# Attention inputs in 2 KB runs, seven warm-up products, no weight piece on ScalarE's queue, and a last expert turned part by part

## The chip, the cores and the metric

The kernel runs on one core of one Trainium2 chip. The metric is the device time of one execution in microseconds (us), as the median over runs. TensorE is called PE, VectorE DVE, ScalarE ACT, GpSimd POOL and SyncE SP, as in the profile.

## The reference

Three layers follow one another on 4 x 576 = 2304 tokens of 512 numbers, all in float32:

```python
def phi(x):                                  # 8 heads of 64, omega is 128 x 64
    proj = np.einsum('bhsd,md->bhsm', x, omega)
    h = proj - np.sum(x * x, axis=-1, keepdims=True) / 2.0
    h = h - np.max(h, axis=-1, keepdims=True)
    return np.exp(h) / np.sqrt(m)
q_p, k_p = phi(q * scale), phi(k * scale)
num = q_p @ (k_p^T v);  den = q_p @ sum(k_p) + 1e-6;  x = num / den

h = x @ w_in;  x = (h - np.tanh(h)) @ w_out      # w_in 512 x 2048, w_out 2048 x 512

logits = x @ w_gate                          # 8 experts, each takes 288 tokens,
                                             # handed out in the order of the logits
out[mask] = np.maximum(x[mask] @ w1[e], 0) @ w2[e]   # w1 512 x 1024, w2 1024 x 512
```

The kernel takes its inputs in a layout that the host makes by copying and turning them alone; w_in and w_out come as 64-bit numbers, since the reference's hold them so.

## The kernel before

The attention goes in 72 steps, called units: for k or q, a granule of two tiles of 128 tokens (or one shared tile, "sh", of two sequences), one half of the heads (hh, four heads) and one head pair. `load_gran` (L390) loads a granule: q and k turned, with the features on the partitions, into a tile `ld`; v into `v1`, whose 65th column per head is set to one by a memset on POOL, so that the sum of k_p comes out of the same product. `unit_ops` (L415) projects it (L436), takes the maximum (DVE, L450), the exponential (ACT, L447), and either adds k_p^T v up in PSUM (L467) or turns q_p (L489) and multiplies (L496). The results are 18 tiles `xt` of 128 tokens.

The MLP goes over six blocks of 384 tokens (three tiles) and 16 chunks of 128 of the 2048 hidden features. float32 accuracy is had from three products of a high and a low part: xH with the high part of w_in, xL with it, and xH with the low part (L611 to L613, in the text M1), then 9 such products per chunk into three accumulators (L658). `weight_ops` (L330) makes these parts from the 64-bit weights: a DMA brings a raw piece of 128 x 512, three steps on DVE (L341, L343, L345) make float32 of it, ACT copies the high part, DVE or POOL subtracts (L305) to get the low part, which is stored to DRAM and read back when a block needs it. `x_ops` (L541) turns an `xt` tile and splits it into xH and xL. The experts follow at about 610 us (`expert_ops`, L1369): gather 288 rows, turn, two layers with the same three products (L1428 to L1430, L1447 to L1449), turn back (L1459) and scatter the rows to the output in three indirect DMAs of POOL.

Nothing of the order is written by hand. Every operation is given to a planner, `Plan` (L66), with a duration and a due time (`plan.at` plus `lag`), and `Plan.run` (L130) puts them out, one at a time, by the earliest start that its own account of the engines, the buffers and the DMA allows, and by due time among equals. Where an operation names two engines, the one that ends earlier by the account is taken; `bias` is added to DVE's end there. Where the account sees PE wait for more than 0.9, `spare` (L1484) puts small products of ones into an accumulator that is not used yet (L1489), for 0.4 of that wait and at most 1.0. Before everything, `warm` (L1478) issues 15 products of 512 columns. The instructions of each engine then run in that order, each waiting for its semaphores.

Names that the text uses: `omega_ops` (L312) loads omega twice, for both halves of the partitions, and scales it on DVE; `bias_ops` (L320) runs two small ACT instructions; LEADX, LEADI, LEADO (L774), WO0 (L1524) and the number in `low_ops` (L1556) are offsets of due times; `end_rows` exists in the changed kernel alone.

## Time and profile before

| | us |
|---|---|
| median of 3 runs | 867.41 |
| lowest and highest run | 864.65, 870.2 |
| the profiled execution | 868.87 |
| its span, first to last instruction | 867.1 |
| PE busy | 839.3 (97%) |
| DVE busy | 651.8 (75%) |
| ACT busy | 470.5 (54%) |
| POOL busy | 272.5 (31%) |

The profile shows one execution. A busy PE is not a PE at its peak: its instructions overlap, and their ends are modelled. In the rows below, "idle before" in square brackets is the time in which the engine had nothing to run, and the name behind the arrow is what ended it. The granted clock is given as a share of full speed: 1.00 is 2.4 GHz and 0.50 is 1.2 GHz. Instructions of PE take 16 entries for eight projections, since each float32 product is done in two passes.

### The profile page before, as it was taken

The numbers are of one execution on the slowest core, as the hardware profiler recorded it, in microseconds if no ns is written. First come the engines' busy times: TensorE is split into PE (matmuls) and PEld (weight loads), VectorE is DVE, ScalarE is ACT, GpSimd is POOL, SyncE is SP. The second block draws the span as 40 slices with busy tenths as digits, with TensorE's granted clock in tenths as the row PEclk, the third lists the DMA queues.
The fourth block names the chain that finished last, engine by engine and source line by source line (L and its number), as shares of the span: only waits on it lengthen the run. The fifth ranks groups of instructions, "written<-read, shape, count | busy, mean of one in ns | idle before, by whom it ended". The sixth has DMA issues, their size and how long they took to land. (4 is left out here: it accounts for less than half of the span.)

```text
span 867.1 us, 17421 instructions
## 1 busy us (share of the span) xinstructions
PE 839.3 (97%) x6126; PEld 750.9 (87%) x6126; DVE 651.8 (75%) x1906; ACT 470.5 (54%) x1024; POOL 272.5 (31%) x292
## 2 busy tenths in 40 slices
PE   7998999999999999999999999999999999999995
PEld 5988888898888888788988996777999999999995
DVE  6979999778777888878878867445878878876720
ACT  4966564655457554565558864013565555554721
POOL 2131343433353345344423334010042142142211
PEclk9989999999999999999999999999999999999998
DMA  8979877977557665743459884668879879779600
GB/s 258 337 261 286 275 250 236 313 257 241 147 178 226 189 207 161 233 141 113 122 191 320 290 300 144 186 219 267 250 221 299 249 211 301 250 193 343 225 28 28
DMA packets 103790, 193.95 MB, mean 224 GB/s; under 512 B 28305, under 2 KB 42257, under 8 KB 103698
## 3 DMA queue, kind: packets, MB, share of 16 engines
q1 hardware_dynamic: 97586, 172.80, 60.5%
q0 software_dynamic: 5664, 18.88, 9.0%
q8 instruction: 49, 0.80, 0.4%
q10 hardware_dynamic: 448, 1.11, 0.4%
q14 instruction: 43, 0.35, 0.1%
HBM read 149.64 MB, written 33.69 MB: 211 GB/s over the span
## 5 line engine op out<-in xcount | busy, mean ns | idle before, releaser
L305 POOL TENSOR_TENSOR gL<-s,gH 128x384 fp32r<-128x384 f32 x68 | 80.0, 1178 | 172.9 <-ACT gH L300 163.7
L611 PE MATMUL bk<-xH,wi 128*128 128x384 f32 x332 | 118.3, 356 | 4.6 <-ACT phi L447 2.7
L739 DVE SCALAR_TENSOR_TENSOR lw<-wf,raw 128x512 f32<-128x512 f32 x128 | 108.9, 850 | 5.3 <-POOL wf L736 2.6
L612 PE MATMUL bk<-xL,wi 128*128 128x384 f32 x332 | 112.1, 338 | 0.0
L613 PE MATMUL bk<-xH,iL 128*128 128x384 f32 x332 | 112.1, 338 | 0.0
L658 PE MATMUL acc<-wo,gL 128*128 128x512 f32 x282 | 111.4, 396 | 0.0
L658 PE MATMUL acc<-wo,gH 128*128 128x512 f32 x240 | 98.8, 412 | 0.0
L658 PE MATMUL acc<-oL,gH 128*128 128x512 f32 x240 | 95.1, 396 | 0.9 <-DVE oL L305 0.8
L447 ACT ACTIVATE phi<-bk,nm 128x128 f32<-128x128 f32 x268 | 75.8, 384 | 32.9 <-DVE nm L450 32.6
L736 POOL TENSOR_TENSOR wf<-oL,wo 128x512 f32<-128x512 f32 x48 | 66.7, 1390 | 38.7 <-DMA oL<-low_wo 36.3
L611 PEld LDWEIGHTS bk<-xH,wi 128*128 128x128 f32 x332 | 63.0, 190 | 11.9 <-ACT phi L447 3.4
L636 DVE SCALAR_TENSOR_TENSOR s<-s,bk 128x384 f32<-128x384 f32 x83 | 45.4, 549 | 33.2 <-ACT s L635 32.8
L615 ACT ACTIVATE s<-bk 128x384 f32<-128x384 f32 x80 | 39.2, 490 | 55.1 <-PE bk L613 49.2
L300 ACT ACTIVATE gH<-s 128x384 fp32r<-128x384 f32 x80 | 42.0, 525 | 46.2 <-DVE s L638 28.1
L612 PEld LDWEIGHTS bk<-xL,wi 128*128 128x128 f32 x332 | 63.1, 190 | 2.8
L658 PEld LDWEIGHTS acc<-wo,gL 128*128 128x128 f32 x282 | 52.9, 188 | 12.3 <-POOL gL L305 0.5
L613 PEld LDWEIGHTS bk<-xH,iL 128*128 128x128 f32 x332 | 62.9, 189 | 0.0
L638 DVE SCALAR_TENSOR_TENSOR s<-s,s 128x384 f32<-128x384 f32 x80 | 55.4, 693 | 0.9
L635 ACT ACTIVATE s<-s,qbias 128x384 f32<-128x384 f32 x80 | 49.3, 616 | 6.3 <-DVE gL L305 1.9
L658 PEld LDWEIGHTS acc<-oL,gH 128*128 128x128 f32 x240 | 45.2, 188 | 7.4 <-DVE oL L305 1.6
L658 PEld LDWEIGHTS acc<-wo,gH 128*128 128x128 f32 x240 | 45.2, 188 | 6.8 <-issue 1.0
L450 DVE TENSOR_REDUCE nm<-bk 128x4 f32<-128x512 f32 (+1 forms) x74 | 45.7, 633 | 6.8 <-PE bk L436 6.2
(413 smaller groups left out, 2320.4 us busy)
## 6 DMA issues: line engine op xcount, KB each, us to landing
r_wraw<-in_moe_w_dram SPq DMA_DIRECT2D x50, 512.0 KB, 5.3
iL<-low_wi SPq DMA_DIRECT2D x80, 256.0 KB, 3.2
oL<-low_wo SPq DMA_DIRECT2D x78, 256.0 KB, 3.1
raw<-in_moe_w_out_dram SPq DMA_DIRECT2D x32, 512.0 KB, 4.3
raw<-in_moe_w_in_dram SPq DMA_DIRECT2D x30, 512.0 KB, 5.2
s_wraw<-in_moe_w_dram SPq DMA_DIRECT2D x14, 512.0 KB, 5.8
dw<-in_moe_w_dram SPq DMA_DIRECT2D x13, 512.0 KB, 5.3
w1l<-dw SPq DMA_DIRECT2D x13, 512.0 KB, 3.0
```

Of the source, the lines that this page charges most:

```text
L305: (nc.gpsimd if e == POOL else nc.vector).tensor_tensor(out, in_, high.bitcast(F32), op=OP.subtract)
L447: nc.scalar.activation(ph.t[:, i0 + i, :], pj.t[:, i * M:(i + 1) * M], AF.Exp, bias=nmx.t[:, i0 + i:i0 + i + 1])
L450: plan.op(DVE, 0.1 + 0.125 * n, lambda e, pj=pj, i0=i0, n=n: V.tensor_reduce(nmx.t[:, i0:i0 + n], pj.t[:, :n * M].rearrange("p (i m) -> p ...
L611: nc.tensor.matmul(ph(), piece(iH, c), xH.t[:, c, :], start=(c == 0), stop=False)
L612: nc.tensor.matmul(ph(), piece(iH, c), xL.t[:, c, :], start=False, stop=False)
L613: nc.tensor.matmul(ph(), piece(iL, c), xH.t[:, c, :], start=False, stop=(c == NC - 1))
L635: plan.op(ACT, 0.52, lambda e: nc.scalar.activation(s.t, ut(), AF.Square, bias=qbias), r=[u], w=[s], lag=2.8)
L636: plan.op(DVE, 0.52, lambda e: V.scalar_tensor_tensor(s.t, s.t, QD, ph(), op0=OP.add, op1=OP.mult), r=[p, s], w=[s], lag=3.4)
L638: plan.op(DVE, 0.65, lambda e: V.scalar_tensor_tensor(s.t, s.t, QC, ut(), op0=OP.mult, op1=OP.mult), r=[u, s], w=[s], lag=4.0)
L658: nc.tensor.matmul(acc[t].t, (gL if k == 2 else gH).t[:, c], (oL if k == 1 else oH).t, start=(f == 0 and k == 0), stop=(f == end and k == ...
L736: plan.op(POOL, 1.45, lambda e: nc.gpsimd.tensor_tensor(w.t, lo.t.bitcast(F32), wo[:, f, :].bitcast(F32), op=OP.add), r=[lo, wbuf["wo", f] ...
L739: x_reads.append(plan.op(DVE, 0.9, lambda e, i=i: nc.vector.scalar_tensor_tensor(scratch.t.bitcast(F32), w.t, 1.0, half(rows[i // 2], i % ...
```

## The change

It has four parts and new numbers for the planner.

The host lays q, k and v out so that what one partition of a granule takes lies in one run: 2 KB for q and k (1 KB for the shared tile), 2080 bytes for v, whose ones are now in the DRAM rows. One DMA loads a granule of v where two did, and the 20 memsets go. omega comes with both halves, in one DMA.

The first two raw pieces of w_in, which went over ACT's queue, go over SP's like the others. The ACT instructions of `bias_ops` no longer share a buffer with omega.

There are 7 warm-up products instead of 15. `spare` is used from a wait of 0.5 on while the planner's time is below 25.

For the last expert, the rows are no longer turned at the end in twelve transposes and three copies of 512 columns: after each of the four quarters of the second layer, `end_rows` copies it and turns it for all three groups of rows, writes the first three quarters out behind the third, and the last quarter in three small pieces.

```diff
-    bias = {"PE": 0.0, "ACT": 0.0, "DVE": 0.6, "POOL": 0.0, "SP": 0.0, "-": 0.0}
+    bias = {"PE": 0.0, "ACT": 0.0, "DVE": 0.66, "POOL": 0.0, "SP": 0.0, "-": 0.0}
-            if e == "PE" and self.fill and t - self.free[e] > 0.9:
+            if e == "PE" and self.fill and t - self.free[e] > (0.5 if t < 25.0 else 0.9):
-                self.dma = max(self.dma, end) + o.nbytes / 280e3
+                self.dma = max(self.dma, end) + o.nbytes / 300e3
-        first = kind == "wi" and f < 2 and not masked
+        first = kind == "wi" and f < 0 and not masked
-            plan.op(POOL, 0.04, lambda e: nc.gpsimd.memset(t.t[:, :n, :, D:], 1.0), w=[t], lag=-6.0)
-            for i in range(n):
-                plan.op(SP, 0.47, lambda e, i=i: nc.sync.dma_start(
-                    t.t[:, i, :, :D], v[(tile + i) * P:(tile + i + 1) * P, hh * HH * D:(hh + 1) * HH * D].rearrange(
-                        "p (h d) -> p h d", d=D)), w=[t], lag=-5.0, nbytes=P * HH * D * 4)
+            W = HH * (D + 1)
+            plan.op(SP, 0.47, lambda e: nc.sync.dma_start(
+                t.t.rearrange("p i h d -> p (i h d)")[:, :n * W], v[b // 2, hh, :, tile % 9 * W:(tile % 9 + n) * W]),
+                w=[t], lag=-5.0, nbytes=P * W * 4 * n)
-    LAG2, LEADX, LEADI, LEADO = 10.35, 14.35, 8.14, 3.98
+    LAG2, LEADX, LEADI, LEADO = 10.35, 4.72, 9.7, 4.85
-                        plan.at = max(x_due[i * TPB + t] + 11.86, start[j - 1] + LEADX)
+                        plan.at = max(x_due[i * TPB + t] + 5.24, start[j - 1] + LEADX)
+    def end_rows(p, d, py, yT):
+        if not d:
+            tails[:] = [(Buf(bank3), Buf(mLr), []) for _ in range(NG)]
+        ends = d == NC - 1
+        cp = None
+        if not ends:
+            plan.op({ACT: 0.3, DVE: 0.37}, 0, lambda e: copy(e, yT.t, py.t[:, :CAP]), r=[py], w=[yT])
+            plan.at += 1.0
+        for g in range(NG):
+            (po, yo, done), n, ix = tails[g], GN[g], idxs[p][g][0]
+            cols = slice(g * GS, g * GS + n)
+            if ends:
+                cp = plan.op((ACT, DVE, ACT)[g], 0.2, lambda e, cols=cols: copy(e, yT.t[:, cols], py.t[:, cols]),
+                             r=[py], wp=[yT])
+            done.append(plan.op(PE, 0.11, lambda e, po=po, n=n, cols=cols: nc.tensor.transpose(
+                po.t[:n, d * P:(d + 1) * P], yT.t[:, cols], ident), rp=[yT], wp=[po],
+                after=([cp] if ends else [yT.writers[-1]]) + done[-1:]))
+            if d >= NC - 2:
+                part = slice(0, d * P + P) if not ends else slice(d * P, DM)
+                w = part.stop - part.start
+                plan.op((ACT, DVE, ACT)[g], 0.1 + 0.001 * w, lambda e, po=po, yo=yo, n=n, part=part: copy(
+                    e, yo.t[:n, part].bitcast(F32), po.t[:n, part]), rp=[po], wp=[yo], after=done[-1:])
+            if ends:
+                plan.op(POOL, 1.1, lambda e, g=g, yo=yo, ix=ix: scatter(g, yo, ix), r=[yo, ix], late=3.5)
-        for i in range(15):
+        for i in range(7):
-    T_UNIT, T_MLP, DUE0, DUE1 = 2.23, 60.95, 7.39, 19.25
+    T_UNIT, T_MLP, DUE0, DUE1 = 2.23, 58.66, 7.39, 19.25
-    WI0, WI1, WO0 = 3.84, 2.4, -13.4
+    WI0, WI1, WO0 = 3.84, 2.4, -10.66
-    low_ops(starts[-2], (NF * steps[-1] + -19.47) / (E * NPRE))
+    low_ops(starts[-2], (NF * steps[-1] + -13.85) / (E * NPRE))
```

The planner's account of each engine also starts at 0.9 to 1.6 instead of 0.

The order on SP, where the kernel begins, of before (ld and v are the granules' tiles, raw a weight piece):

```order
L405 DMA ld_173<-in_k_dram 128x2x256
L399 DMA v_175<-in_v_dram 128x4x64 x2
L405 DMA ld_189<-in_k_dram 128x2x256
L399 DMA v_177<-in_v_dram 128x4x64 x2
L405 DMA ld_195<-in_k_dram 128x2x128
L399 DMA v_179<-in_v_dram 128x4x64
L339 DMA raw_198<-in_moe_w_in_dram 128x1024
L405 DMA ld_200<-in_k_dram 128x2x256
```

And of the changed kernel, the same place on SP:

```order
L404 DMA ld_157<-in_k_dram 128x512
L398 DMA v_162<-in_v_dram 128x520
L404 DMA ld_173<-in_k_dram 128x512
L398 DMA v_176<-in_v_dram 128x520
L339 DMA raw_178<-in_moe_w_in_dram 128x1024
L339 DMA raw_180<-in_moe_w_in_dram 128x1024
L404 DMA ld_182<-in_k_dram 128x256
L398 DMA v_185<-in_v_dram 128x260
```

The two raw pieces came from ACT's queue; they now stand behind the first two granules of k and v and ahead of the third.

The order on DVE, where its work begins, of before (nm are the maxima of a projection in a bank bk or rx, wf the float32 weights):

```order
L315 TENSOR_SCALAR omT<-omT 128x128
L341 TENSOR_SCALAR wf_215<-raw_187 128x512
L343 SCALAR_TENSOR_TENSOR wf_215<-raw_187,wf_215 128x512
L450 TENSOR_REDUCE nm_230<-bk_205 128x4
L450 TENSOR_REDUCE nm_232<-bk_206 128x4
L345 SCALAR_TENSOR_TENSOR wf_215<-raw_187,wf_215 128x512
L450 TENSOR_REDUCE nm_247<-bk_218 128x4
L341 TENSOR_SCALAR wf_266<-raw_191 128x512
L450 TENSOR_REDUCE nm_275<-rx_219 128x4
```

And of the changed kernel, the same place on DVE:

```order
L315 TENSOR_SCALAR omT<-omT 128x128
L451 TENSOR_REDUCE nm_201<-bk_189 128x4
L451 TENSOR_REDUCE nm_215<-bk_190 128x4
L451 TENSOR_REDUCE nm_222<-bk_205 128x4
L451 TENSOR_REDUCE nm_240<-rx_206 128x4
L341 TENSOR_SCALAR wf_247<-raw_178 128x512
L343 SCALAR_TENSOR_TENSOR wf_247<-raw_178,wf_247 128x512
L345 SCALAR_TENSOR_TENSOR wf_247<-raw_178,wf_247 128x512
L341 TENSOR_SCALAR wf_272<-raw_180 128x512
```

The four maxima of the first two granules moved ahead of the first weight piece.

The order on PE at its end, of before (s_yT are the quarters of the last expert's result, bd and be banks):

```order
L1449 MATMUL bd_17105<-s_hH_17044,s_ewL_16843 128x288
L1459 MATMUL bd_17134<-ident,s_yT_17064 128x128
L1459 MATMUL bd_17134<-ident,s_yT_17082 128x128
L1459 MATMUL bd_17134<-ident,s_yT_17109 128x128
L1459 MATMUL bd_17134<-ident,s_yT_17132 128x128
L1459 MATMUL be_17139<-ident,s_yT_17064 128x128
```

And of the changed kernel, from the third quarter's transposes among the products of the fourth on:

```order
L1487 MATMUL bd_17121<-s_hH_16931,s_ewL_16742 128x288
L1396 MATMUL bd_17076<-ident,s_yT_17125 128x128
L1396 MATMUL be_17078<-ident,s_yT_17125 128x128
L1396 MATMUL be_17080<-ident,s_yT_17125 32x128
L1485 MATMUL bd_17121<-s_hH_16948,wi 128x288
L1486 MATMUL bd_17121<-s_hL_16953,wi 128x288
```

Nine of the twelve transposes moved ahead of the last product; behind it stand the three of the last quarter.

## Rows read from the trace of the kernel before

**Rows 1.** The page, part 1: busy time, share of the span, instructions.

```profile
PE 839.3 (97%) x6126; PEld 750.9 (87%) x6126; DVE 651.8 (75%) x1906; ACT 470.5 (54%) x1024; POOL 272.5 (31%) x292
```

**Rows 2.** Busy time by stage: length, engines with instructions, PE clock, DMA share, GB/s.

```profile
0.00:50.00 50.00, 43.31 (x394) 36.20 (x394) 39.52 (x92) 35.23 (x109) 12.03 (x23) 0.97 0.98 309
50.00:60.00 10.00, 9.72 (x72) 9.46 (x72) 6.36 (x12) 6.31 (x17) 2.20 (x3) 0.82 0.55 180
60.00:136.00 76.00, 71.38 (x479) 63.07 (x480) 72.08 (x132) 47.05 (x120) 24.85 (x23) 1.00 0.83 265
...
610.00:835.00 225.00, 224.72 (x2070) 217.36 (x2069) 175.53 (x776) 126.97 (x211) 61.58 (x81) 1.00 0.79 244
```

**Rows 3.** Timeline of the start, PE: start, duration, line, tiles, count, idle before.

```profile
1.65 5.47 PE L1480 MATMUL bk<-onev 128*128 128x512 bf16 x15 [1.65 <-DVE onev L251]
...
7.05 1.16 PE L436 MATMUL bk<-omT,ld 64*128 64x128 f32 x16
...
10.59 0.37 PE L436 MATMUL bk<-omT,ld 64*128 64x128 f32 x1 [2.38 <-DMA ld<-in_k_dram]
...
11.68 0.76 PE L1489 MATMUL kv<-onev 128*128 128x128 bf16 x10
```

**Rows 4.** Timeline of DVE, 5 to 50 us.

```profile
8.73 0.43 DVE L341 TENSOR_SCALAR wf<-raw 128x512 uint32<-128x512 uint32 x1 [3.39 <-DMA raw<-in_moe_w_in_dram]
9.19 0.69 DVE L343 SCALAR_TENSOR_TENSOR wf<-raw,wf 128x512 uint32<-128x512 uint32 x1
9.80 1.28 DVE L450 TENSOR_REDUCE nm<-bk 128x4 f32<-128x512 f32 x2
...
16.77 1.64 DVE L345 SCALAR_TENSOR_TENSOR wf<-raw,wf 128x512 uint32<-128x512 uint32 x1
...
49.09 0.69 DVE L305 TENSOR_TENSOR xL<-bk,xH 128x512 fp32r<-128x512 f32 x1 [0.80 <-ACT xH L300]
```

**Rows 5.** DMA issues of the span: tiles, queue, count, size, median us to landing.

```profile
raw<-in_moe_w_in_dram SPq DMA_DIRECT2D x30, 512.0 KB, 5.2
...
ld<-in_k_dram SPq DMA_DIRECT2D x16, 256.0 KB, 5.0
...
omT<-in_omega_dram ACTq DMA_DIRECT2D x2, 32.0 KB, 3.4
```

**Rows 6.** Busy time in a stretch of 2 us, columns as in rows 2.

```profile
48.00:50.00 2.00, 1.44 (x8) 1.04 (x6) 1.20 (x3) 1.54 (x6) 0.96 (x1) 0.50 0.96 350
```

**Rows 7.** Timeline of PE where the MLP starts.

```profile
49.84 0.69 PE L611 MATMUL bk<-xH,wi 128*128 128x384 f32 x1 [0.56 <-DVE xL L305]
...
53.74 0.33 PE L611 MATMUL bk<-xH,wi 128*128 128x384 f32 x1
...
55.84 1.89 PE L467 MATMUL kv<-v,phi 128*128 128x65 f32 x16
```

**Rows 8.** What PE waited for, 60 to 136 us: total, times, longest.

```profile
PE bk L611 <- DVE xt L509: 1.3, 1, 1.3
```

**Rows 9.** Groups of DVE: count, busy, mean ns, idle before.

```profile
L305 DVE TENSOR_TENSOR gL<-s,gH 128x384 fp32r<-128x384 f32 x12 | 8.1, 673 | 3.1 <-ACT gH L300 3.1
...
L305 DVE TENSOR_TENSOR lw<-wf,wi 128x512 fp32r<-128x512 f32 x4 | 3.8, 953 | 0.0
```

**Rows 10.** Timeline of POOL, 12 to 32 us.

```profile
16.42 1.45 POOL L305 TENSOR_TENSOR lw<-wf,wi 128x512 fp32r<-128x512 f32 x1 [1.18 <-ACT wi L300]
```

**Rows 11.** Timeline of the end, 853 to 868 us.

```profile
855.39 0.49 PE L1459 MATMUL bd<-ident,s_yT 128*128 128x128 f32 x3
855.65 0.41 ACT L300 ACTIVATE s_yT<-bd 128x288 f32<-128x288 f32 x1 [2.77 <-PE bd L1449]
...
856.48 0.60 ACT L300 ACTIVATE mL<-bd 128x512 f32<-128x512 f32 x1 [0.42 <-PE bd L1459]
...
857.36 0.98 POOL L1463 DMA_INDIRECT out_dram<-mL,r_ix  x1 [22.87 <-ACT mL L300]
...
858.64 0.96 POOL L1463 DMA_INDIRECT out_dram<-mL,r_ix  x1 [0.21 <-issue]
```

More of the change, by code (lines that the diff above doesn't have):

```diff
@@ L70 @@
     CROSS, SAME = 0.2, 0.13
-    bias = {"PE": 0.0, "ACT": 0.0, "DVE": 0.6, "POOL": 0.0, "SP": 0.0, "-": 0.0}
+    bias = {"PE": 0.0, "ACT": 0.0, "DVE": 0.66, "POOL": 0.0, "SP": 0.0, "-": 0.0}
     def __init__(self):
         self.ops, self.n, self.at = [], 0, 0.0
-        self.free = dict.fromkeys(("PE", "ACT", "DVE", "POOL", "SP", "-"), 0.0)
+        self.free = {"PE": 1.6, "ACT": 0.9, "DVE": 1.5, "POOL": 1.2, "SP": 0.9, "-": 0.0}
         self.dma = 0.0
@@ L191, in tile_kernel @@
     nc = tc.nc
-    D, M = omega.shape
+    D, M = omega.shape[0] // 2, omega.shape[1]
     P = 128
-    NT, DM = v.shape
+    NT, DM = out.shape
     H = DM // D
@@ L310, in tile_kernel @@
     bT = Buf(None)
+    bBias = Buf(None)
     def omega_ops():
-        for i in range(2):
-            plan.op(ACT, 0.6, lambda e, i=i: nc.scalar.dma_start(omT[i * D:(i + 1) * D, :], omega), w=[bT], nbytes=P * D * 4)
+        plan.op(ACT, 0.6, lambda e: nc.scalar.dma_start(omT, omega), w=[bT], nbytes=P * M * 4)
         plan.op(DVE, 0.2, lambda e: nc.vector.tensor_scalar(omT, omT, 1.0 / math.sqrt(math.sqrt(D)), None, op0=OP.mult),
@@ L321, in bias_ops @@
         for x in (pbias, qbias):
[L322 removed]
+            plan.op(ACT, 0.8, lambda e, x=x: nc.scalar.activation(x, x, AF.Copy), w=[bBias])
     HMIN = 2.0 ** -15 * 1.125
@@ L429, in unit_ops @@
             two = held_pj[nm, b, g, hh] = Buf(bank, early=early), Buf(bank, early=early)
+            lv = lambda: ld.t.rearrange("p a n -> p (a n)").rearrange("p (a n) -> p a n", n=P if sh else 2 * P)
             def proj(e):
@@ L435, in proj @@
                             rows, i = slice(c * D, (c + 1) * D), 2 * r + a
-                            nc.tensor.matmul(two[c].t[:, i * M:(i + 1) * M], ld.t[rows, a, r * P:(r + 1) * P], omT[rows],
+                            nc.tensor.matmul(two[c].t[:, i * M:(i + 1) * M], lv()[rows, a, r * P:(r + 1) * P], omT[rows],
                                              start=True, stop=True)
@@ L1367, in tile_kernel, with scatter @@
     sc_prev = []
+    def scatter(g, yo, ix):
+        nc.gpsimd.memset(spacer, 0.0)
+        st = nc.gpsimd.indirect_dma_start(
+            out=out, out_offset=bass.IndirectOffsetOnAxis(ap=ix.t[:GN[g]].bitcast(U32), axis=0),
+            in_=yo.t[:GN[g]].bitcast(F32), in_offset=None)
+        for x in sc_prev:
+            tc.declare_no_dep(st.ins, x.ins, reason="every token has one expert")
+        sc_prev.append(st)
+    tails = []
+    def end_rows(p, d, py, yT):
[22 more added lines that the diff above has]
+                plan.op(POOL, 1.1, lambda e, g=g, yo=yo, ix=ix: scatter(g, yo, ix), r=[yo, ix], late=3.5)
     def expert_ops(p):
@@ L1450, in expert_ops @@
                 o = plan.op(PE, 0.40, mm, r=[H, L, hH, hL], w=[py], after=[o] if o else [])
+            if p == E - 1:
+                end_rows(p, d, py, yT)
+                continue
             plan.op({ACT: 0.3, DVE: 0.37}, 0, lambda e, py=py, yT=yT: copy(e, yT.t, py.t[:, :CAP]), r=[py], w=[yT])
             ys.append(yT)
+        if p == E - 1:
+            return
         plan.at = base + AT_OUT
@@ L1459, in transposes @@
                     nc.tensor.transpose(po.t[:GN[g], d * P:(d + 1) * P], ys[d].t[:, g * GS:g * GS + GN[g]], ident)
-            def scatter(e, g=g, yo=yo, ix=ix):
-                nc.gpsimd.memset(spacer, 0.0)
-                st = nc.gpsimd.indirect_dma_start(
-                    out=out, out_offset=bass.IndirectOffsetOnAxis(ap=ix.t[:GN[g]].bitcast(U32), axis=0),
-                    in_=yo.t[:GN[g]].bitcast(F32), in_offset=None)
-                for x in sc_prev:
-                    tc.declare_no_dep(st.ins, x.ins, reason="every token has one expert")
-                sc_prev.append(st)
             plan.op(PE, 0.44, transposes, r=ys, w=[po])
             plan.op({ACT: 0.48, DVE: 0.6}, 0, lambda e, g=g, po=po, yo=yo: copy(e, yo.t[:GN[g]].bitcast(F32), po.t[:GN[g], :]), r=[po], w=[yo])
-            plan.op(POOL, 1.1, scatter, r=[yo, ix], late=3.5)
+            plan.op(POOL, 1.1, lambda e, g=g, yo=yo, ix=ix: scatter(g, yo, ix), r=[yo, ix], late=3.5)
     plan.at = -30.0
@@ L1478, in warm @@
     def warm(e):
-        for i in range(15):
+        for i in range(7):
             nc.tensor.matmul(idle.t, onev.to_broadcast([P, P]), onev.to_broadcast([P, DM]), start=True, stop=True)
-    plan.op(PE, 6.0, warm, w=[idle])
+    plan.op(PE, 3.0, warm, w=[idle])
     def spare(us):
@@ L1664, in _lay_out @@
 def _lay_out(np, name, a):
-    if name in ("omega", "moe2_w_gate_t"):
+    if name == "omega":
+        return np.concatenate((a.T, a.T), 0)
+    if name == "moe2_w_gate_t":
         return a.T
@@ L1677, in _lay_out @@
     a = np.concatenate((a[:, 0], a[:, 1, e:], a[:, 1, :e]), 1)
-    return a.reshape(B * S, H * D) if name == "v" else a.transpose(0, 2, 1)
+    if name == "v":
+        a = np.concatenate((a.reshape(B // 2, -1, 128, H, D), np.ones((B // 2, 2 * S // 128, 128, H, 1), a.dtype)), 4)
+        return a.reshape(B // 2, -1, 128, 2, H // 2 * (D + 1)).transpose(0, 3, 2, 1, 4).reshape(B // 2, 2, 128, -1)
+    a = a.transpose(0, 2, 1).reshape(B // 2, 2, 2, 128, 2 * S).transpose(0, 1, 3, 2, 4)
+    cuts = (0, 256, 512, 640, 896, 1152)
+    return np.concatenate([a[..., i:j].reshape(B // 2, 2, 128, -1) for i, j in zip(cuts, cuts[1:])], 3)
 def _in_order(np, x, S=576):
```

5 lines of the change are left out of this document (2 added, 3 removed).

## The prediction

> **What bounds the kernel now.** I read the page first: TensorE (PE) is busy in 97% of the span [rows 1], so some 28 us hold no product, and only these, products that do no work and half-rate stretches can be won. The table of stages says where they lie [rows 2]: 6.7 us in the first 50, 4.6 us between 60 and 136, only 0.3 us between 610 and 835; the rest is short waits between and the drain behind the last product. Then the timelines. At the start [rows 3] the 15 warm-up products from 1.65 take 5.5 us, the first projection follows at 7.05 and takes 1.16 us, and the second stands 2.4 us for its k tile. VectorE (DVE) idles 3.4 us until the first raw weight piece lands at 8.73; from there it is nearly full until the third low part of x at 49.09 [rows 4], behind which the first product of the MLP (L611) starts at 49.84 [rows 7]. DVE has 39.5 us of work in the first 50 us [rows 2], so from 8.73 on DVE sets when the MLP starts. From there PE itself sets the pace, except for its waits between 60 and 136, in which DVE is busy 72.1 of 76 us.
>
> **The start.** The loads carry the same bytes (v a little more, for its ones); they are issued in other pieces and another order. SP's queue now begins k, v, k, v, raw, raw in six issues, where it held k, v, v, k, v, v; ScalarE's queue issues omega once and no raw piece. PE: at the row's spacing seven products end at 4.2 to 4.7 (15 took 5.47 us, the last of them closer together than the first, so the first seven took up to 3.0) instead of 7.04. Omega lands 3.4 us behind an issue at 0.9 [rows 5]: 4.3. The first k tile, issued at 0.9 too, lands at 5.9 by the median of 5.0 us [rows 5]; with next to nothing queued ahead of it, it can come as omega does, at 4.3. I take 5.3 for the first projection, between the two. Its 1.16 us put DVE's first reduction at 6.5. The four reductions that now stand ahead of the weights need 2.6 us (two take 1.28 [rows 4]), until 9.1; the first raw piece, fifth in SP's queue and so issued near 2.7, needs 5.2 us [rows 5] and is there at 7.9: no second wait. DVE's full stretch then starts at 6.5 instead of 8.73, 2.2 us earlier. Against that DVE does one weight piece more ahead of the third low part of x (0.43 + 0.69 + 0.69 = 1.8 us [rows 4]), and one low part of a weight (0.95 [rows 9]) and one copy less: 0.7 us net. So the MLP starts 1.5 us earlier. Bounds: 0, if the k tile needs its 5.9 and DVE is held up by 0.9 us more; -2.8, if the k tile is there at 4.3 and the extra piece fills holes. I take **-1.5**.
>
> **The clock.** The granted clock is 0.50, the lower of its two levels, between 48 and 50 [rows 6]. Twelve products of L611 to L613 from 49.84 take 3.9 us there, the next twelve, from 53.74 to 55.84, 2.1 us [rows 7]: 1.8 us lost on the path. The changed order puts nine warm products right ahead of the first L611, and 18 some 36 products later. Whether the level still falls no row can say; bounds -1.8 and 0. No row is nearer to the one end, and I take the middle, **-0.9**.
>
> **The waits behind the start.** The planner's DVE bias of 0.66 moves 13 subtractions from DVE to GpSimd (POOL): four low parts of weights, nine of the hidden layer; seven of them stand before 136 us. These seven free 4 x 0.95 + 3 x 0.67 = 5.8 us of DVE [rows 9]. But POOL needs 1.45 us for one [rows 10], and a two-input DVE step beside it is stretched: 1.64 us at 16.77, while POOL's subtraction runs from 16.42, against 0.69 at 9.19 with POOL idle [rows 4, 10]. If half of the seven meet such a step, that gives back 3.3 us, if all, 6.7. I reckon with half: 2.5 us less DVE work where PE waits 4.6 us. The leads (x 4.72 instead of 14.35, low parts of w_in 9.7 instead of 8.14, of w_out 4.85 instead of 3.98, x transposes of later blocks 6.6 us earlier) change order, not work; they bring loads and transposes forward, which bears on the longest of these waits, 1.3 us at DVE xt [rows 8]. I take **-2.0** for all of it; bounds -4.6 (every wait of 60 to 136) and +2.1 (seven stretches of 0.95 us against seven savings of some 0.65).
> On this the Trainium skill, page "SBUF — State Buffer", section "SBUF: two separate sides", states that the port pair which VectorE and GpSimd share is an exclusive lock, held for a whole instruction, and no division of bandwidth. The step at 16.77 agrees. By the rule taken strictly a subtraction moved to GpSimd wins nothing wherever a two-input step stands beside it, and the sum comes out above the time before (the third case below).
>
> **The extra products.** The order has 62 small warm products where it had 10: 27 ahead of the first L611, in waits for DVE, at no cost; 35 behind it, among the first eight chunks. Ten took 0.76 us [rows 3], so 35 cost 2.7 us if PE would not have waited there (it is busy 9.7 of the 10 us from 50 to 60 [rows 2]), and nothing if it would. The planner sets them where it sees a wait of more than 0.9 us, and fills four tenths of it. Nearer to that than to a full PE, I take **+1.0**.
>
> **The end.** For the last expert the transposes of the first three quarters of the rows go ahead of the last products. PE has no gap in that stage [rows 2], so nine transposes at 0.11 us (three take 0.49, of which the last one 0.27 [rows 11]) push the last product back by 1.0 us; before, three of them ran in the shadow of a copy. The first scatter stood at 857.36, 1.97 us behind 855.39, where PE was through with its products. Now: 0.26 us to ScalarE's start, 0.27 for 128 columns (on the line through 0.41 at 288 and 0.60 at 512), some 0.3 for DVE's piece, which ScalarE's 32-column piece waits for and which so stands ahead of the last copy, 0.2 for that piece, 0.27 for the copy, 0.28 to POOL: 1.6 us. The other two scatters follow at POOL's own 1.28 us [rows 11]. So +1.0 - 0.4 = **+0.6**; bounds -0.4 (the transposes cost nothing) and +1.0 (the chain behind them is no shorter).
>
> Twenty memsets of POOL and 16 issues of SP go; neither engine is waited for there, so nothing. Sum: -1.5 - 0.9 - 2.0 + 1.0 + 0.6 = -2.8 us. The profiled execution took 868.87 us for its span of 867.1; the median of the three runs is 867.41, 1.46 us below it and inside their spread of 864.65 to 870.2. From the median: **864.6 us**.
>
> **Rivals.** Second: the clock holds and the added products lie in real waits. Then -1.5 - 1.8 - 4.6 + 0 + 0.6 = -7.3, 860.1 us. For it speaks that between 60 and 136 DVE and PE are both within 6% of full, so a little less DVE work counts fully; against it, that the longest wait there is for the attention's own scaling, which the change leaves on DVE.
> Third: the lock paces. POOL's seven more subtractions cost DVE 2.1 us more than they save, and only the start is won: -1.5 + 2.1 + 0.6 = +1.2, 868.6 us. For it, the 1.64 us step; against it, that a subtraction on POOL is stretching only where a two-input step runs beside it, and reductions and scalings lie between.
> Fourth, slower than before: the planner's waits are not the chip's. The 35 products stand in PE's stream between the chunks of the first block where PE is full and cost their 2.7 us; no wait behind goes: -1.5 + 2.7 + 0.6 = +1.8, 869.2 us. It decides from 12 such products on (0.9 us, what start and end leave). For it, PE's 9.7 of 10 us; against it, that fewer attention products now lie between those chunks, so PE comes sooner to weights that DVE still has to make.
> That seven warm products leave PE at the lower level for the first projections would be the change not doing what it says: a projection of 1.16 us then takes 2.3, the start gives 0.4, and the time is 865.7 us, inside the forecast's range.
>
> **How the numbers follow.** Forecast 0.48 (its own range 862.5 to 867), second 0.25, third 0.12, fourth 0.15. The range takes in the second and the fourth, with the start's -2.8 below the one and the end's +1.0 and the 0.3% spread of the runs above the other: 858.5 to 870.5. A measurement of this kernel tells about 1%, 8.7 us, from no change. Faster by more needs the second case with the start at its bound and a wait or two elsewhere: 0.10. Slower by more needs the third and fourth together and more, for which I see no row: 0.04. The rest is 0.86.
>
> **What would show it.** Right: DVE's first reduction before 7 us, and no wait for a k tile at the second projection; the first L611 at 48 to 48.6; PE idle less than 4 us in the 76 us from 60 on; the last expert's products 1 us longer, and 1.6 us from there to the first scatter. Wrong: a first L611 at 49.8 or later; a granted clock of 0.50 for longer than from 46 to 54, above all before 20 us; DVE's two-input weight steps often at 1.6 us; a PE without gaps around the added products.

## The result, and the profile after

In the comparison that the prediction is held to, four executions of each kernel, the changed kernel took 876.11 us (874.62 to 881.41), the kernel before 868.81 us (864.65 to 871.28): a ratio of 1.0113, 95% interval 1.007 to 1.0156. The forecast was 864.6 us, and the range ended at 870.5. Two later sets of the same kernel, on two chips (runs c9 and c16 below), gave 1.0060 (1.0029 to 1.0091) and 1.0078 (1.0045 to 1.0111). The three intervals overlap; weighted by their widths they give 1.008, so the change costs some 6.8 us. One execution of c9 and four of c12, which took 889 to 926 us at granted clocks of 0.84 to 0.97, are left out of all ratios and mean clocks below.

The profiled execution after took 874.62 us, its span 872.8, 5.7 us more than the 867.1 before. Part 1 of its page:

```profile
PE 845.4 (97%) x6170; PEld 757.4 (87%) x6170; DVE 652.7 (75%) x1892; ACT 472.7 (54%) x1031; POOL 284.9 (33%) x284
```

PE is busy 6.1 us longer than in [rows 1], in a span 5.7 us longer, so by the page the lost time is not waiting. It is no more work either: products at the lower level of the clock take longer, and since their ends are modelled, a short wait of PE can lie hidden in its busy time. The table of stages, with columns as in [rows 2], shows part of it:

```profile
0.00:50.00 50.00, 44.39 (x387) 39.31 (x387) 40.01 (x84) 33.71 (x102) 12.34 (x15) 0.90 0.86 290
50.00:60.00 10.00, 8.78 (x55) 8.78 (x55) 8.56 (x16) 7.56 (x21) 1.29 (x1) 0.83 0.82 259
60.00:136.00 76.00, 71.39 (x499) 61.79 (x500) 72.25 (x121) 44.45 (x109) 35.80 (x26) 1.00 0.85 272
136.00:530.00 394.00, 392.73 (x2522) 349.67 (x2519) 311.90 (x707) 238.83 (x550) 162.56 (x143) 1.00 0.65 212
610.00:835.00 225.00, 223.74 (x2053) 214.63 (x2051) 176.37 (x781) 126.03 (x211) 57.42 (x75) 1.00 0.80 244
...
18.00:22.00 4.00, 3.54 (x31) 3.48 (x33) 3.96 (x7) 3.79 (x15) 1.29 (x1) 0.82 1.00 339
22.00:26.00 4.00, 4.00 (x23) 3.77 (x20) 3.47 (x6) 3.03 (x10) 1.28 (x1) 0.50 0.97 348
26.00:30.00 4.00, 4.00 (x26) 3.40 (x25) 2.34 (x5) 2.03 (x6) 0.70 (x1) 0.50 1.02 375
30.00:34.00 4.00, 4.00 (x44) 3.85 (x44) 3.18 (x5) 3.09 (x11) 0.57 (x1) 0.90 0.96 323
```

Two things are to be seen. In the first 50 us the granted clock is 0.90 where it was 0.97: from about 20.5 to 31 us it is at 0.50, the lower level, and in the 4 us from 22 PE gets through 23 instructions. And between 60 and 136 us nothing changed: PE is busy 71.39 us as before, DVE 72.25, while POOL works 11 us more.

The timeline of the start, PE, then DVE (answers to [rows 3, 4 and 7]):

```profile
2.00 3.17 PE L1514 MATMUL bk<-onev 128*128 128x512 bf16 x7 [2.00 <-DVE onev L251]
5.09 2.11 PE L437 MATMUL bk<-omT,ld 64*128 64x128 f32 x17
...
18.46 1.10 PE L468 MATMUL kv<-v,phi 128*128 128x65 f32 x8 [0.76 <-ACT kvs L300]
...
51.22 1.54 PE L560 MATMUL bk<-ident,xt 128*128 128x128 f32 x6 [3.96 <-DVE xt L510]
...
54.89 0.42 PE L612 MATMUL bk<-xH,wi 128*128 128x384 f32 x1
```

```profile
7.13 1.89 DVE L451 TENSOR_REDUCE nm<-bk 128x4 f32<-128x512 f32 x3 [3.37 <-PE bk L437]
...
28.35 0.69 DVE L451 TENSOR_REDUCE nm<-bk 128x4 f32<-128x512 f32 x1 [1.66 <-PE rx L437]
...
48.09 1.55 DVE L345 SCALAR_TENSOR_TENSOR wf<-raw,wf 128x512 uint32<-128x512 uint32 x1
```

The start does much of what the prediction said: seven products, no wait for the second k tile, DVE at work 1.6 us earlier than in [rows 4] (2.2 were reckoned). Then, in the half-rate stretch, DVE waits for PE (28.35), and the first L612 stands at 54.89, 5.05 us behind the first L611 of [rows 7]. PE's wait of 3.96 us for the third xt belongs to the new order: c1, c9, c14 and c16 below, which have no such stretch, have it too. The end, with the last product of the last expert, the copies and the first scatter (answers to [rows 11]):

```profile
861.51 0.29 PE L1487 MATMUL bd<-s_hH,s_ewL 128*128 128x288 f32 x1
861.84 0.28 ACT L300 ACTIVATE s_yT<-bd 128x128 f32<-128x128 f32 x1 [1.73 <-PE bd L1487]
...
862.57 0.27 ACT L300 ACTIVATE mL<-bd 128x128 f32<-128x128 f32 x1
...
863.11 0.97 POOL L1372 DMA_INDIRECT out_dram<-mL,r_ix  x1 [23.33 <-ACT mL L300]
```

The lag against the profile before is 5.05 us at the first L612, only 2.58 at the first product of the experts (605.86 before, 608.44 after), and 6.25 at their last one (855.26 and 861.51). The experts' stage, from the first 128x288 product to the last, takes 253.07 us where it took 249.40. The prediction had 1.0 us for that stage.

### The profile page after: what moved, and what is told of

Read it like the earlier page. It is cut to its first block, busy times and chain, and to the rows that moved or that the text cites. A ratio compares the mean times of both kernels' runs of the same rounds, so it can differ in the third digit from the quotient of the medians.

```text
span 872.8 us, 17440 instructions
## 1 busy us (share of the span) xinstructions
PE 845.4 (97%) x6170; PEld 757.4 (87%) x6170; DVE 652.7 (75%) x1892; ACT 472.7 (54%) x1031; POOL 284.9 (33%) x284
## 5 line engine op out<-in xcount | busy, mean ns | idle before, releaser
L305 POOL TENSOR_TENSOR gL<-s,gH 128x384 fp32r<-128x384 f32 x74 | 85.5, 1155 | 193.4 <-ACT gH L300 187.5
L612 PE MATMUL bk<-xH,wi 128*128 128x384 f32 x332 | 117.7, 355 | 0.5 <-DVE s L637 0.5
L612 PEld LDWEIGHTS bk<-xH,wi 128*128 128x128 f32 x332 | 62.5, 188 | 6.5 <-DVE s L637 0.7
L639 DVE SCALAR_TENSOR_TENSOR s<-s,s 128x384 f32<-128x384 f32 x80 | 57.8, 723 | 0.9
## 6 DMA issues: line engine op xcount, KB each, us to landing
iL<-low_wi SPq DMA_DIRECT2D x80, 256.0 KB, 3.3
oL<-low_wo SPq DMA_DIRECT2D x78, 256.0 KB, 3.1
```

Of the source, the lines that this page charges most:

```text
L305: (nc.gpsimd if e == POOL else nc.vector).tensor_tensor(out, in_, high.bitcast(F32), op=OP.subtract)
L612: nc.tensor.matmul(ph(), piece(iH, c), xH.t[:, c, :], start=(c == 0), stop=False)
L639: plan.op(DVE, 0.65, lambda e: V.scalar_tensor_tensor(s.t, s.t, QC, ut(), op0=OP.mult, op1=OP.mult), r=[u, s], w=[s], lag=4.0)
```

## The experiments

All runs in one table: the ratio to the kernel before on the same chip, the mean granted clock over a run's executions (that of before on that chip in brackets), and from the profile the first L611 (or L612) and the length of the experts' stage, both in us.

| run | ratio (95%) | clock | first L611 | experts |
|---|---|---|---|---|
| c1 old end | 1.0069 (1.0044 to 1.0095) | 0.987 (0.992) | 50.84 | 256.0 |
| c2 layout and start alone | 1.0173 (1.0138 to 1.0208) | 0.980 (0.992) | 59.22 | 249.1 |
| c3 numbers alone | 1.0174 (1.0142 to 1.0207) | 0.981 (0.992) | 63.72 | 254.3 |
| c4 changed, 15 warm | 1.0123 (1.0094 to 1.0152) | 0.986 (0.992) | 56.11 | 252.7 |
| c5 before, new end | 0.9995 (0.9969 to 1.0022) | 0.992 (0.990) | 49.99 | 250.0 |
| c6 before, 7 warm | 1.0028 (1.0003 to 1.0052) | 0.989 (0.990) | 49.90 | 249.0 |
| c7 old end, no filling | 1.0091 (1.0060 to 1.0122) | 0.984 (0.990) | 53.87 | 252.9 |
| c8 old end, more filling | 1.0075 (1.0047 to 1.0103) | 0.990 (0.990) | 50.71 | 253.5 |
| c9 changed again | 1.0060 (1.0029 to 1.0091) | 0.989 (0.991) | 48.91 | 259.0 |
| c10 before, bias 0.66 | 1.0102 (1.0067 to 1.0137) | 0.988 (0.991) | 57.16 | 252.9 |
| c11 before, new leads | 1.0008 (0.9983 to 1.0032) | 0.992 (0.991) | 50.73 | 255.7 |
| c12 before, raw on SP | 1.0045 (1.0010 to 1.0080) | 0.989 (0.991) | 56.04 | 253.9 |
| c13 before itself | 0.9987 (0.9962 to 1.0012) | 0.992 (0.991) | 54.96 | 249.2 |
| c14 experts' order of before | 1.0026 (0.9997 to 1.0056) | 0.990 (0.991) | 49.71 | 250.7 |
| c15 c14 with 15 warm | 1.0048 (1.0021 to 1.0075) | 0.989 (0.991) | 51.67 | 250.7 |
| c16 changed, third time | 1.0078 (1.0045 to 1.0111) | 0.988 (0.991) | 50.25 | 254.9 |
| c17 before, experts' order of after | 1.0043 (1.0014 to 1.0072) | 0.989 (0.990) | 50.42 | 252.4 |
| c18 new leads, experts' order of before | 0.9987 (0.9962 to 1.0012) | 0.992 (0.990) | 50.83 | 249.1 |

**The end (c1, c5).** First I asked which half of the lag is the end's. c1 is the changed kernel without `end_rows`, c5 the kernel before with it (and with `scatter` taken out of `expert_ops`, as in the diff of the change):

```diff
-            if p == E - 1:
-                end_rows(p, d, py, yT)
-                continue
```

> The changed kernel, but the last expert's rows turned as in the kernel before (twelve transposes and three copies of 512 columns behind the last product); all else is the changed kernel's, and so is the order up to the last expert. Theory A (the start lost it): the turning part by part costs what its transposes cost, 0.6 to 1 us, so about 875.3, and the first L612 comes at 54.9 as in the changed kernel. Rival E (the end lost it): the 3.2 us that the stage behind 608 us grew by belong to it, so 872.9.

> The kernel before with the changed kernel's turning of the last expert's rows part by part, and nothing else; the order up to the last expert is that of the kernel before. Theory E (the end lost it, by the difference between the changed kernel and the one with the old end, about 0.4%): 3 to 4 us slower than before. Rival, the step of the prediction: nine transposes ahead of the last product, a shorter chain behind it, 0.6 us slower, and at most 1.0.

c1 is 0.4% under the first ratio of the changed kernel, which spoke for E; c5 says otherwise. In an order that is the old one up to the last expert, the new end moves the time by -0.4 us (0.9995 of 867.4), with an interval of -2.7 to +1.9. The experts' stage grows by 0.6 us, from 249.40 to 250.0. Theory E falls; the extra microseconds of that stage are not the end's.

**The parts alone (c2, c3, c10, c11, c12).** c2 has the new layout and start with the old numbers and the old end; c3 the old kernel with all new numbers:

```diff
-    bias = {"PE": 0.0, "ACT": 0.0, "DVE": 0.6, "POOL": 0.0, "SP": 0.0, "-": 0.0}
+    bias = {"PE": 0.0, "ACT": 0.0, "DVE": 0.66, "POOL": 0.0, "SP": 0.0, "-": 0.0}
...
-    LAG2, LEADX, LEADI, LEADO = 10.35, 14.35, 8.14, 3.98
+    LAG2, LEADX, LEADI, LEADO = 10.35, 4.72, 9.7, 4.85
```

> The changed kernel's layout, raw pieces on SyncE's queue and seven warm-up products, with the planner's numbers and the end of the kernel before. Theory A1 (the half-rate stretch at 21 to 31 us comes from the new start, whatever the planner's numbers): a granted clock of 0.50 for some 10 us between 18 and 34, first product of the MLP at 53 or later, 872 to 876. Rival A2 (the planner's numbers put VectorE's weight steps ahead of xt): no such stretch, first product of the MLP at 48 to 49.5, 866 to 868.

> The kernel before with nothing but the changed kernel's planner numbers (bias 0.66, the account's starting values, the filling rule, 300e3, the leads, T_MLP, WO0, the number of low_ops). A1: the clock at 18 to 34 stays at 1.00, the first product of the MLP within 1 us of 49.84, 867 to 869.5. A2: VectorE does weight steps ahead of xt, PE waits 3 us or more there, first product at 53 or later, 872 to 876.

Each half alone is 1.7% slower, which is beyond both ranges that had been expected, and both together 0.7 to 0.8% (c1, c16): the numbers seem to belong to this list of operations. Of the 15 us some 7 go with the lower clock of these two runs, by the 0.61 us per 0.001 found below. In c3 the stretch at half rate, in the table of stages, lasts from 12 to 36 us, and PE, full all the time, lets DVE do 7.13 us of work in 16:

```profile
14.00:18.00 4.00, 4.00 (x21) 4.00 (x20) 3.93 (x9) 3.12 (x11) 0.60 (x2) 0.50 0.86 301
18.00:34.00 16.00, 16.00 (x102) 14.97 (x102) 7.13 (x12) 7.13 (x24) 3.94 (x6) 0.50 0.89 264
```

A1 and A2 are both too simple, since the stretch comes with either half (and, as c13 below shows, with neither). Then the numbers one by one, in the kernel before (c10: only the bias; c11: only the leads), and the raw pieces alone:

```diff
-        first = kind == "wi" and f < 2 and not masked
+        first = kind == "wi" and f < 0 and not masked
```

> The kernel before with VectorE's bias in the planner at 0.66 instead of 0.6, the order up to the first MLP blocks unchanged. The step of the prediction: subtractions moved from VectorE to GpSimd save about 2 us of PE's waits, so 0.998. Theory W (the new numbers bring waits of PE for r_cond into the experts' stage, 2 to 3 us): that stage grows from 249.4 to 252 or more, ratio 1.002 or above.

> The kernel before with the changed kernel's leads alone (LEADX 4.72, LEADI 9.7, LEADO 4.85, x transposes of later blocks 5.24), the order ahead of the first L611 unchanged. If the leads bring the stretch between 351 and 605 us from 253.8 to 251, as the changed kernel's traces have it, the ratio is 0.997; if they also bring the waits for r_cond, 1.000 to 1.003, with the experts' stage at 252 or more.

> The kernel before with the first two raw pieces on SyncE's queue instead of ScalarE's, the old layout, 15 warm products and the old numbers. Theory S (any new operation list at the start, planned with numbers that were fitted to another, puts VectorE's steps in a worse order): first L611 at 52 or later, ratio 1.005 to 1.015. Rival (the layout is what spoils the old numbers' order): first L611 within 1 us of 49.9, ratio within 0.3% of 1.

The bias alone costs 1.0% where I had counted it as a gain, though POOL has only five instructions more (297 against 292). PE is idle for 6.7 us between 136 and 530 us in c10, and for 2.2 to 3.9 in the profile before, c5, c6, c13 and c17. Two of its waits, which the kernel before does not have there, show what kind of thing comes of the bias:

```profile
PE acc L658 <- POOL oL L305: 1.5, 1, 1.5
...
PE bk L559 <- DVE s L636: 0.7, 1, 0.7
```

The leads alone change nothing that can be measured (they too give the experts another order, a third one), and the raw pieces alone cost 0.45%. These three ran on a chip where the kernel before takes 871.9 us, and there the experts' stage was 253.9 us in c12 too, whose order behind the MLP is that of before. So the chip has a say in that stage, and the question of order or chip had to be put on one chip.

**The experts' order (c13, c14, c16, c17).** At the end of the MLP the planner sets every engine of its account to one time and goes on. That time is 1474.7 in the kernel before and 1466.6 in the changed one, and bias and DMA rate differ; of PE's 2269 rows from the first 128x288 product on, 916 stand elsewhere because of it (the rows outside the longest common sequence of the traces of before and c17). c14 sets the account back there, which gives exactly the old order (with the new end, as in c5); c17 does the reverse in the kernel before and gives exactly the new one, with the old end (as in c1).

```diff
-    now = max(plan.free.values())
+    now, plan.dma = 1474.6967714286225, 1452.4389428571906
+    plan.bias = dict(plan.bias, DVE=0.6)
+    plan.rate = 280e3
```

> The kernel before, unaltered, for a profile on the same chip as the next three. Theory W (order): its experts' stage takes 249 to 250 us with PE idle under 0.5 us, as on the chips before. Rival V (chip): where the chip is one of the slower ones (before at 871 or above), 252 us or more with 2 us or more of waits, with this order too. The time is that of before, ratio 1.000.

> The changed kernel once more, on the same chip as the three runs before this one, for its profile: experts' stage 253 us or more with PE idle 0.9 us or more by theory W, and by at least 2.5 us longer than that of the kernel before here; by rival V as long as that within 1 us. Ratio 1.006 to 1.011.

> The changed kernel, with the planner's account set back, at the end of the MLP, to the kernel before's (bias 0.6, 280e3, its time and DMA time): up to there the changed kernel's order, behind it that of before with the rows turned part by part. Theory W: the experts' stage falls from 253 or more to 249 to 250.5, the ratio from 1.007 to 1.003 or less. Rival V: stage and ratio stay within 1 us and 0.1% of the changed kernel's.

> The kernel before up to the end of the MLP; there the planner's account is set to the changed kernel's (bias 0.66, 300e3, its time and DMA time), which gives the experts' stage the changed kernel's order, with the old end. Theory W: the stage grows from 249.2 to 252.5 to 255 us, with PE waiting for r_cond and r_cmp, ratio 1.003 to 1.006 at an unchanged mean clock. Rival (the 4.5 us need the changed kernel's start as well): stage below 250.5, ratio within 0.2% of 1.

On one chip, with the first and the last 128x288 product from the timelines, c13 (the kernel before):

```profile
608.65 0.38 PE L1399 MATMUL bd<-r_sel,mH 128*128 128x288 f32 x1
...
857.83 0.30 PE L1449 MATMUL bd<-s_hH,s_ewL 128*128 128x288 f32 x1
```

c16 (the changed kernel):

```profile
606.81 0.38 PE L1437 MATMUL bd<-r_sel,mH 128*128 128x288 f32 x1
...
861.71 0.29 PE L1487 MATMUL bd<-s_hH,s_ewL 128*128 128x288 f32 x1
```

c14 (the changed kernel with the old order):

```profile
605.50 0.38 PE L1438 MATMUL bd<-r_sel,mH 128*128 128x288 f32 x1
...
856.16 0.29 PE L1488 MATMUL bd<-s_hH,s_ewL 128*128 128x288 f32 x1
```

249.2, 254.9 and 250.7 us: the changed kernel comes to the experts 1.8 us earlier than the kernel before and leaves them 3.9 us later. With the old order behind the MLP the ratio falls from 1.0078 to 1.0026, 4.5 us of 866.7, and c17 shows 0.43%, 3.7 us of 868.0 (1.2 to 6.2 by its interval), from the new order alone, without any other part of the change. Of the 4.5 us some 1.6 go with the clock, which is 0.0027 higher in c14's executions than in c16's; the stages themselves, 4.2 us apart, ran at 1.00 in both. The other profiles bear it out. Leaving out c9 to c12, which share the slower chip, the six further ones with the old order (before, c2, c5, c6, c15, c18) have a stage of 249.0 to 250.7 us, and the six with the new one (after, c1, c3, c4, c7, c8) one of 252.7 to 256.0. Theory W stands. c14 keeps the changed kernel's start and end; what is left, 0.26%, cannot be told from no change.

Where such a microsecond arises is read from the timelines of c16 around PE's longest wait there:

```profile
647.59 1.06 ACT L300 ACTIVATE wi<-r_wraw 128x1024 fp32r<-128x1024 f32 x1 [2.44 <-DMA r_wraw<-in_moe_w_dram]
648.55 0.39 ACT L1470 ACTIVATE s_hH<-be 128x288 fp32r<-128x288 f32 x1
...
646.19 0.17 DVE L1110 SCALAR_TENSOR_TENSOR r_thr<-r_d,r_base 128x16 int32<-128x16 int32 x1
648.97 0.46 DVE L1471 SCALAR_TENSOR_TENSOR s_hL<-be,s_hH 128x288 fp32r<-128x288 f32 x1 [2.60 <-ACT s_hH L1470]
649.35 0.52 DVE L1117 TENSOR_TENSOR r_cmp<-r_m,r_thr 128x160 bf16<-128x160 f32 x2
...
649.72 0.45 PE L1123 MATMUL rp<-r_cmp,pairs 128*128 128x32 bf16 x9 [1.66 <-DVE r_cmp L1117]
```

r_cmp, a step of the search that picks the next expert's tokens, has its input at 646.4. But the new order puts a low part s_hL ahead of it on DVE; that waits for s_hH on ACT, which stands behind the copy of a weight piece whose DMA has not landed. One late load holds ACT, DVE and PE. c9 has the same chain with a wait of 2.16 us at its end; in the profile after and in c17 PE has no wait for r_cmp. In c14 r_cmp follows r_thr at once, ahead of that s_hL, and PE has no such wait:

```profile
644.75 0.17 DVE L1111 SCALAR_TENSOR_TENSOR r_thr<-r_d,r_base 128x16 int32<-128x16 int32 x1
644.96 0.53 DVE L1118 TENSOR_TENSOR r_cmp<-r_m,r_thr 128x160 bf16<-128x160 f32 x2
645.54 0.46 DVE L1472 SCALAR_TENSOR_TENSOR s_hL<-bd,s_hH 128x288 fp32r<-128x288 f32 x1
```

So one part of the loss differs between executions of one order, with the load: c16's stage is 1.8 us longer than the 253.1 of the profile after, as much as this one place holds it up (c9's 259.0 us come from the slower chip as well). The rest are short waits, most of them for r_cond; in c17:

```profile
PE rp L1148 <- DVE r_cond L1144: 1.1, 3, 0.5
```

PE's idle time in the stage, 1.5 us in c17 and 2.8 in c16, shows only part of the loss, since the modelled end of the product ahead covers the first 0.3 us or so of each wait. From start to start, c17 has seven places where PE's next product is more than 0.3 us off (0.13 is usual), 3.5 us together, and c16 nine with 5.4; c18, on c17's chip with the old order, has none, and c13 one of 0.3.

**Clock, warm products and filling (c4, c6, c7, c8, c9, c15).** The half-rate stretch of the profile after looked like the cause of the late first L612, and in that execution it most likely is. But c1, c8, c9, c14 and c16 have the same order up to there, small warm products aside, and none of them has the stretch; their first L612 stands between 48.91 and 50.84. c7, without those products, has it (53.87). c13, the kernel before, does have one:

```profile
12.00:14.00 2.00, 2.00 (x15) 2.00 (x12) 2.00 (x4) 2.00 (x8) 1.31 (x1) 0.50 1.08 329
14.00:18.00 4.00, 4.00 (x22) 3.66 (x22) 2.72 (x6) 1.76 (x6) 0.47 (x2) 0.50 0.64 206
18.00:22.00 4.00, 4.00 (x26) 3.88 (x27) 1.74 (x2) 1.14 (x3) 0.97 (x2) 0.50 0.81 215
```

and its first L611 is at 54.96. The stretch belongs to an execution and not to the kernel. How much the clock matters is seen over all 300 executions, 24 sets of one kernel on one chip: within a set, 0.001 less of mean granted clock goes with 0.61 us more (standard error 0.02). On one chip the kernel before alone runs from 862.3 us at a clock of 0.997 to 873.0 at 0.982.

> The changed kernel itself, unaltered, for more executions beside the experiments. If its turning part by part costs nothing, as in the kernel before (ratio 0.9995), its ratio is that of the first experiment, 1.007 to 1.009; if it costs 3 us here, 1.011 again. Theory C (clock): its runs' mean clock lies at 0.985 to 0.988, some 0.005 below that of the kernel before.

c9 came out under the lower of the two ratios that it was to choose between, with a clock 0.003 under that of before. Whether the products at the start govern the clock was asked five times: 15 warm products in the changed kernel (c4, where other planner results moved with it) and, in an unchanged order, 7 in the kernel before (c6) and 15 in c14 (c15); no small products (c7) and more than twice as many (c8):

```diff
-            if e == "PE" and self.fill and t - self.free[e] > (0.5 if t < 25.0 else 0.9):
-                self.fill(min(0.4 * (t - self.free[e]), 1.0))
+            if e == "PE" and self.fill and t - self.free[e] > (0.2 if t < 64.0 else 0.9):
+                self.fill(min((0.9 if t < 64.0 else 0.4) * (t - self.free[e]), 3.0))
```

> The changed kernel with 15 warm-up products instead of 7. A1 in the form that too few warm products lower the clock: no 0.50 between 18 and 34; the start comes some 2 us later, but the 4 to 5 us at half rate go, first L612 at 51 to 53, 872.5 to 874.5. A1 in the form that the order behind them lowers it, and A2: the stretch stays, first L612 at 55 or later, 876 to 878.

> The kernel before with 7 warm-up products instead of 15, the order of all else unchanged. Theory C (a start with little work for PE lets the granted clock fall behind it): the runs' mean clock falls from about 0.994 to 0.988 or less, and the time is 2 to 5 us longer. Rival: the clock stays, the second projection still waits for its k tile, and VectorE for its first raw piece, so no change within 1 us.

> The changed kernel with the old end (as in the first experiment), and none of the 62 small warm products; the order of all else is that kernel's. Theory C: without them PE has less work ahead of the first L612, the mean clock falls below that kernel's 0.988, and the time rises by 2 us or more, to 874 or above beside a before of 866.8. Rival F (the products cost what they take, up to 2.7 us for the 35 behind the first L612): 870 to 871.5 at an unchanged clock.

> The changed kernel with the old end, and the filling rule raised up to the planner's time of 64 (from a wait of 0.2 on, nine tenths of it, at most 3 us), 139 small warm products instead of 62; the order of all else is that kernel's. Theory C: the mean clock rises to 0.993 or more, and the time falls by 2 to 4 us, to 868 to 870 beside a before of 866.8. Rival F: the clock stays at 0.988, and the added products cost 1 to 4 us, 873 to 876.

> The kernel of the last run with 15 warm-up products, the order of all else unchanged. Theory C (the clock of the runs is set by PE's work at the start, the eight products among it): mean clock up by 0.003 or more, time 1 to 2 us shorter, ratio at or below 1.000. Rival: the clock stays, and the first projection starts 2 us later than 5.1; 1 to 2 us slower.

In c4 the stretch stays, from 23.0 to 33.2 us, the first L612 comes at 56.11 and the time is 876.62 us, as the second form said. In c15 the clock stays (0.989 against 0.990), the first L612 comes 1.96 us later, and the ratio is 0.22% higher: the rival. In c6 the clock stays as well, and the time is still 0.28% longer, which none of my readings explains. With the filling the clock seems to rise, 0.984 without (six executions), 0.987 with 62 products (eight, on another chip), 0.990 with 139 (eight), but no time is seen to be won: the ratio is 1.0091, 1.0069 and 1.0075, with intervals that overlap. Both signs of theory C came in c7, by the point estimates; in c8 the clock stayed under its 0.993, and the time did not fall. Theory C stays open for the filling, and falls for the products at the start.

**A version under both?** c18 takes the new leads and the old experts' order:

> The kernel before with the changed leads (LEADX 4.72, LEADI 9.7, LEADO 4.85, 5.24), and the experts' order of before. If the leads win 1 to 2.5 us between the first L611 and the experts, and the order behind costs nothing, 0.997 to 0.9985. If the gain there was only the absence of a half-rate stretch at 531 us, 1.000.

0.9987, interval 0.9962 to 1.0012; 868.08 beside 868.03 us. No version that I tried is faster than the kernel before by more than its interval.

## Why the prediction was wrong

**The start, -1.5: right on DVE, lost again on PE.** DVE's first reduction came at 7.13 us in the profile and at 6.30 in c9 (predicted 6.5), and no k tile was waited for. In the four executions without an early stretch and with the unaltered filling (c1, c9, c14, c16) the third low part of x ends at 48.7 us on average; with the start of before and no early stretch ([rows 4], c5, c11, c17, c18) it ends at 50.3. These are the 1.5 us. But the first L612 of the four stands at 49.93 on average and the first L611 of the five at 50.36, a gain of only 0.4. In the old order the first product follows 0.05 us behind that low part, in the new one 0.9 to 1.3 us behind it, since PE is not through with its own stream. In c14 the third low part, the first of the two in the second line, ends at 48.37:

```profile
47.18 1.81 PE L469 MATMUL kv<-v,phi 128*128 128x65 f32 x8
...
47.69 1.28 DVE L306 TENSOR_TENSOR xL<-bk,xH 128x512 fp32r<-128x512 f32 x2
...
48.78 1.16 PE L1524 MATMUL kv<-onev 128*128 128x128 bf16 x9
...
49.71 0.67 PE L613 MATMUL bk<-xH,wi 128*128 128x384 f32 x1
```

Eight products of the attention and nine small warm ones stand ahead of the first product of the MLP, at a granted clock of 0.50 (47.2 to 49.7 us). In c7, without the small ones, it follows 0.2 us behind the third low part, in c8, with 22 of them there, 1.9 us. So the step that failed in this term is DVE as the only engine that sets when the MLP starts.

DVE's two-input weight steps were stretched more often as well. In c9 six of them ahead of the third low part of x take 1.2 to 1.7 us, before four do, and in both every one of these stands beside a subtraction of POOL; in the profile after, the step at 48.09 stands beside this:

```profile
47.25 1.84 POOL L305 TENSOR_TENSOR lw<-wf,wi 128x512 fp32r<-128x512 f32 x1 [2.89 <-DMA low_wi<-lw]
```

Two more long steps are 1.5 us more work, but DVE's holes shrank by about as much: from its start to the end of the third low part it takes 41.7 us in c9 and 41.05 before. The Trainium skill, page "SBUF — State Buffer", section "SBUF: two separate sides", has VectorE, in a step with two inputs in SBUF, and a GpSimd instruction that reads SBUF locking each other out for a whole instruction. The trace agrees for these steps; two short steps in c9 also overlap a subtraction, but they began first, and the subtraction beside the first of them took 1.66 us, where the shortest in that stretch took 1.26.

**The clock, -0.9: moved, not held.** The level still falls ahead of the first L612, in c1, c9, c14 and c16 between 43.4 and 46.1 us, during PE's wait of 3.96 us for the third xt or up to 0.6 us behind it, and for 3.4 to 6.8 us. It ends 0.5 to 1.8 us behind the first L612, where it ends 3.5 to 4.2 us behind the first L611 in the profile before, c5, c17 and c18 (in c11 ahead of it); but now the products ahead of the first L612, which PE must get through, run at it. No run separates what the one won from what the other lost.

**The waits behind the start, -2.0: 0.** PE's idle time from 60 to 136 us is 4.6 us in both first profiles, and DVE's work there did not shrink by 2.5 us: it is 72.25 us, where it was 72.08. The wait at DVE xt of [rows 8] went, and one for phi came:

```profile
PE kv L468 <- ACT phi L448: 2.3, 2, 1.2
```

Behind 136 us something was won instead, up to 530: 1.3 us idle, where the kernel before has 3.9 in its first profile and 2.6 in c13. c10 shows that the bias by itself loses.

**The extra products, +1.0: in another place.** The nine right ahead of the first L612, reckoned at no cost, delay it by 1.1 us (1.3 behind the third low part in c1, 0.2 in c7). What all 62 cost to the end is not shown: c7 leaves them out and is no faster than c1, but its clock is 0.004 lower, which by 0.61 us per 0.001 is worth 2.4 us.

**The end, +0.6: its parts came.** The stage grew by 0.6 us (c5, against the profile before), the first scatter follows 1.60 us behind the start of the last product, where it was 2.10 (855.26 to 857.36), a gain of 0.5 where 0.4 was predicted, and c5 as a whole cannot be told from 0.

Three of the signs that I had named for a wrong prediction came, a first L612 behind 49.8, a longer stretch at 0.50 and two-input weight steps often at 1.6 us; the first profile put them on one page, and none was the main cause.

**What failed** is the step that is not in the sum. "[Rows 2]: PE has no gap in that stage" was read as a property of the experts' stage, and of the numbers I wrote that they "change order, not work"; I followed that order only up to 136 us. The gapless stage was a property of one order, which the planner makes anew from a time in its account. The new order costs 3.7 to 4.5 us (c17, c14), more than the sum of all terms that I had. The rest of the 6.8 us, some 2 to 3, stays open: it lies within c14's interval of 1.0026 (0.9997 to 1.0056). The fourth rival named the mechanism, the planner's waits are not the chip's, but put it into the first MLP block and bounded it by 2.7 us.

## What to carry to other kernels

Where a planner writes the order, a changed number reaches every stage that is planned after it; compare the orders to the end of the program, and treat each stage that is free of waits now as something the change can lose. A run with the old order from one point on, and one with only the new order from there, split such a loss cleanly, where undoing one part of the change does not: here each half alone was slower than both together. Where one engine is said to set when a stage starts, look at what the next engine still has in its own stream ahead of the awaited instruction. Before a stretch in one profile is called the cause, look for it in a second execution of either kernel, and set times beside the mean granted clock.

## What had not been expected of the hardware

The granted clock can sit at 0.50 for 10 to 24 us while PE is nearly full: in the profile after from 20.5 us on, behind one wait of 0.76 us, for 10.2 us, in c13 from 12 us on for 13.7, in c3 for 23.9. The same order has the stretch in one execution and not in another. The Trainium skill, page "TensorE: Matmul & The Clock Gate", section "Part 1: The HAM clock gate (the "warmup" mystery)", says of a start that the number of slow products varies from run to run of one kernel; the traces here show such a difference from run to run 12 to 31 us into the program too.

And one chip took 871.9 us for the kernel before at a mean clock of 0.991, where three others took 866.7 to 868.0 at 0.990 to 0.992: 3.9 to 5.2 us that the clock does not explain. On it the experts' stage took 253.9 us (c12) in the order that needs 249.0 to 249.4 elsewhere.
